# A fused attention and maxout kernel: evictions and filler dealt by engine clocks, q and k of batch 1 turned on TensorE

## The chip, the core and the metric

The kernel runs on one core of a Trainium2 chip. The core has TensorE (PE in the profile; its weight loads are PEld), VectorE (DVE), ScalarE (ACT), GpSimd (POOL) and SyncE (SP). Matrix products go from SBUF through TensorE into PSUM banks, and VectorE or ScalarE copies ("evicts") them to SBUF. SP's queue issues nearly all DMAs in program order. The metric is device time in microseconds (us). Three runs of the kernel before gave 203.61, 203.33 and 203.15 us, a median of 203.33 us.

## The reference

Attention with a causal mask over 4 batches, 8 heads, 768 positions and a head size of 64. Each head is either a full ("retrieval") head or a streaming head that sees 4 sink positions and a window of 64. The result goes through a maxout layer.

```python
scores = scale * np.matmul(q, k.transpose(0, 1, 3, 2))
scores = np.where(mask[None], scores, -1e9)      # causal, or causal & (sink | window)
a = np.exp(scores - scores.max(-1, keepdims=True))
a = a / (a.sum(-1, keepdims=True) + 1e-9)
x = np.matmul(a, v).transpose(0, 2, 1, 3).reshape(B * S, H * D)   # 3072 x 512
h1, h2 = x @ w1, x @ w2                          # 512 x 1024 each
out = np.maximum(h1, h2) @ w_out                 # 3072 x 512
```

## The kernel before, in words

**Pairs and chunks.** Two heads of one batch make a pair: 16 pairs, n = 0 to 15, four per batch (HP = 4). A pair's causal 6x6 block triangle is cut into six chunks (`CHUNKS`), so there are 96 chunks, t = 6n + c. For a chunk, `scores` (L282, matmuls at L296) fills one buffer of two PSUM banks, `expo` (L317) takes the exponential on ScalarE, `mask` (L328, from batch 1 on) multiplies on VectorE, and `weighted` (L348, matmuls at L359) multiplies with v. Five chunks of a pair have exponentials over 128x1024; c = 3 has 128x256. There are two score buffers, so the scores of chunk t+2 wait for the exponential of chunk t. When half a pair is complete, `normalise` (L368) divides on VectorE into the tile `x`.

**q, k, v.** `load_pair` (L189) issues three loads of 384 KB on SP's queue. q and k are cast to bf16 (`cast_qk`, L253) and transposed into `qkt`. This is done in one of two ways. `turn` (L209) makes six transposes on TensorE into a PSUM bank and one eviction. `turn_qk` (L262, the DMA at L267) is one DMA transpose on SP's queue. Pairs below `LONG` (L134, HP + 2 = 6) take the first way and also load q and k with six rows of a head side by side per partition (L183); pairs from 6 on take the second and load in rows of 64 elements (L176). `x` of batch 0 is transposed by TensorE, `x` of batches 1 to 3 by DMA (`turn_x`, L277).

**The maxout layer** uses max(h1, h2) = h2 + relu(h1 - h2): `w12` = w1 - w2 (`diff_w`, L565) and `w2o` = w2 @ w_out are formed on the chip. For each half of a batch (384 positions) `up` (L389, matmuls at L394) is one of eight units of 4 matmuls with an eviction into `g` (relu, L163 on VectorE, L167 on ScalarE), and `down` (L401, matmuls at L411) is one of three units of 12 matmuls with an eviction into `ot` and a store (L419). `w2o` needs `w2t`, the transpose of w2: eight units `prep_w2t` (L536) of four transposes and an eviction, and four units `prep_w2o` (L545).

**Order.** The schedule is written out by the program itself (`manual_schedule`); each engine executes its instructions in that order. Batch 0 runs through 24 chunks. Then come the sixteen `up` units of batch 0 with the eight `prep_w2t` between them (L707 to L734), while TensorE turns q and k of pair 4. Then a loop (L757 on) takes two chunks per step, "a group": scores of t+2 and t+3, `expo(t+2)`, `weighted` of t-2 and t-1, `side(t)`, half a budget of filler, `expo(t+3)`, `mask(t+2)`, `side(t+1)`, the other half of the filler, `mask(t+3)`.

**Side work.** `side` (L643) issues loads, casts, turns and DMA transposes at fixed chunks. For pairs that are turned on TensorE in this part: the casts at c = 5 two pairs ahead (q on VectorE, k on GpSimd), and the two turns at c = 0 and c = 1 of the pair before. For the others: both casts on GpSimd at c = 2 and `turn_qk` at c = 4, both two pairs ahead. From batch 1 on a `load_pair` is issued four pairs ahead at c = 4 or three ahead at c = 0, and `turn_x` of the previous pair at c = 4 (or c = 0), just ahead of `turn_qk`.

**Filler.** `fill` (L497) runs queued units until a budget of TensorE time is used: `cost()` of what is queued, divided by the groups left, where the first pair of the next batch counts as part of a batch's groups. `step` (L476) chooses between `turns`, `shorts` (`up`) and `longs` (`prep_w2o`, `down`, in four parts). Two PSUM banks serve them; a bank counts as free again `EVACUATED` = 1.1 us of planned TensorE time after its unit.

**Who evicts.** `evac` (L157) takes VectorE when the sum of estimated VectorE times given so far is not above that of ScalarE. `vec` and `sca` add to these sums, and L706 sets both to zero where batch 0's attention ends.

Of the kernel before, what the change touches and what calls it, by code (L numbers as in the profile page):

```python
# [49 lines left out]
def kernel(  # L50
# [82 lines left out]

    LONG = HP + 2  # L134
    NV = 3
# [10 lines left out]

    given = {"v": 0.0, "s": 0.0}

    def vec(us):
        given["v"] += us  # L150
        return nc.vector

    def sca(us):
        given["s"] += us
        return nc.scalar

    def evac(out, in_, cols, relu=False, on_vector=None):  # L157
        if on_vector is None:
            on_vector = given["v"] <= given["s"]
        if on_vector:  # L160
            eng = vec(0.16 + cols / 960)
            if relu:
                eng.tensor_scalar_max(out=out, in0=in_, scalar1=0.0)  # L163
            else:
                eng.tensor_copy(out=out, in_=in_)  # L165
        else:
            sca(0.2 + cols / 1300).activation(  # L167
                out=out, in_=in_, func=ACT.Relu if relu else ACT.Copy
            )

# [146 lines left out]
    def expo(t):  # L317
        n, c = chunk(t)
        s = st[n]
        w = 128 * len(CHUNKS[c][0])  # L320
        at = atp.tile([128, 2, 4, 128], BF16, tag="at", name="at")
        sca(0.13 + 2 * w / 1300).activation(  # L322
            out=at.rearrange("p h e c -> p h (e c)")[:, :, 0:w],
            in_=s["ps", c][:, :, 0:w], func=ACT.Exp, scale=scale,
        )
        s["at", c] = at

    def mask(t):  # L328
# [19 lines left out]
    def weighted(t):  # L348
        n, c = chunk(t)
        s = st[n]  # L350
        at = s["at", c]
        for hh in range(2):
            for e, (j, i) in enumerate(CHUNKS[c][0]):
                half, col = divmod(i, 3)
                first = ("po", half) not in s
                if first:
                    s["po", half] = psum_o.tile([128, 2, 3, D + 1], F32, tag="po", name="po")
                rhs = s["vb"][:, hh, j, :] if i - j < 2 else s["vf"][:, hh, j, :]
                nc.tensor.matmul(  # L359
                    s["po", half][:, hh, col, :], lhsT=at[:, hh, e, :], rhs=rhs,  # L360
                    start=first, stop=(c == done(n, half)),
                    skip_group_check=True,
                )
# [4 lines left out]
    def normalise(n, half):  # L368
        s = st[n]
        po = s["po", half]  # L370
        if half == 0:
            s["x"] = work.tile([128, NB, 2, D], BF16, tag="x", name="x")
        rez = work.tile([128, 2, 3], F32, tag="rez", name="rez")
        vec(0.2).reciprocal(out=rez, in_=po[:, :, :, D])  # L374
        vec(0.55).tensor_tensor(  # L375
            out=s["x"][:, 3 * half:3 * half + 3].rearrange("p i h d -> p h i d"),
# [61 lines left out]
    PART = 3  # L438
    plan = {"pe": 0.0, "owe": 0.0}
    free = [0.0, 0.0]  # L440
    busy = [False, False]
    turns, shorts, longs = [], [], []
    current = []
    EVACUATED = 1.1

    def spend(us):
        plan["pe"] += us

# [4 lines left out]
    def run_short(queue):  # L453
        e = pick_bank()
        us, f, _ = queue.pop(0)
        spend(us)
        f((bank_a, bank_d)[e])
        free[e] = plan["pe"] + EVACUATED
        return us

    def run_long():
        if not current:
            e = pick_bank()
            busy[e] = True
            current.extend([longs.pop(0), e, 0])
        (us, f, _), e, part = current
        spend(us)
        f(part, (bank_a, bank_d)[e])
        current[2] += 1
        if current[2] == 12 // PART:  # L470
            busy[e] = False
            free[e] = plan["pe"] + EVACUATED
            current.clear()
        return us

    def step():  # L476

        e = pick_bank()
        open_ = e is not None and free[e] <= plan["pe"]
        pend = [u[2] for u in longs] + ([current[0][2]] if current else [])  # L480
# [54 lines left out]

    def prep_w2t(fc, bank):  # L536
        pw = bank("pw").bitcast(BF16)[:, 0:512]
        for kc in range(KC):
# [3 lines left out]
            )  # L542
        evac(w2t[:, fc, :], pw, 270)

# [136 lines left out]
    for t in range(T0):  # L681
        if t + 2 < T0:
            scores(t + 2)
            expo(t + 2)
            spend(0.8)
        if t > 0:
            weighted(t - 1)
            spend(0.4)
        if t + 1 < T0:
# [25 lines left out]
    for n in range(HP + 1, HP + 4):  # L715
        load_pair(n)
    n = HP
    for e, u in enumerate(first_ups):
        u[1](banks.pop(0))
        if e == 1:  # L720
# [28 lines left out]
    longs += downs(0, 0) + downs(0, 1)  # L749
    scores(T0)  # L750
    scores(T0 + 1)
    expo(T0)
    expo(T0 + 1)
    mask(T0)
    mask(T0 + 1)
    for t in range(T0, T + 2, 2):
        b, p = pairs[min(t, T - 1) // NCH]  # L757
        if t + 2 < T:
            scores(t + 2)
            scores(t + 3)  # L760
            expo(t + 2)
            spend(0.7)
        if t > T0:
            weighted(t - 2)
            weighted(t - 1)
            spend(0.5)
        if t >= T:
# [91 lines left out]
```

## Time and profile before

The profiled execution took 203.91 us; its span is 202.1 us.

| engine | busy us | share of the span |
|---|---|---|
| PE | 187.7 | 93% |
| ACT | 112.3 | 56% |
| DVE | 108.5 | 54% |
| PEld | 105.5 | 52% |
| POOL | 67.9 | 34% |

TensorE's mean granted clock is 0.983. DMA moved 37.09 MB. In the chain of work that ended last, PE has 63%, DMA 16% and ACT 8% of the span.

How to read it: a row of the timeline has a start, a duration (of several instructions together, with "xN"), the engine, the line, the operation, out<-in, and in square brackets the idle time of the engine before it and what ended that. Rows of SP are DMA issues: their duration is the time SP's queue spent on the issue, waits included, and not the transfer. A row of the windows has a stretch, its length, then the busy time of PE, PEld, DVE, ACT and POOL with the number of instructions, the granted clock of TensorE, the share of the DMA engines and GB/s. A row of the grouped lines has the busy time and the mean ns of one, then the idle time ahead.

### The profile page before, as it was taken

Reading aid. Unit: us, or ns where it says so; the run is one execution under the profiler, and the core shown is the slowest. Engines: PE = TensorE matmul, PEld = TensorE weight load, DVE = VectorE, ACT = ScalarE, POOL = GpSimd, SP = SyncE. Lnnn points to the kernel's source line nnn. Section 1 sums busy time; section 2 is a strip of 40 time slices with the busy share of each in tenths; the row PEclk is TensorE's granted clock in tenths of the full one; section 3 lists DMA queues with packets and bytes.
Section 4 is the critical chain, followed back from the end, with each engine's and each line's share of the span. In section 5 each row is a group of like instructions: output and inputs, shape, how many; then the busy total and the mean of one; then the engine's idle time right before and its main releaser. Section 6 shows DMA issues by size and latency. Waiting matters only on the chain.

```text
span 202.1 us, 4504 instructions
## 1 busy us (share of the span) xinstructions
PE 187.7 (93%) x1856; PEld 105.5 (52%) x1856; DVE 108.5 (54%) x205; ACT 112.3 (56%) x151; POOL 67.9 (34%) x74
## 2 busy tenths in 40 slices
PE   7799998997999999579999999999999999999993
PEld 2366665575455555354555455554555645554452
DVE  1767667986776775826383737664623632232110
ACT  2789895589667667661747455935454630532110
POOL 1478349981764451507154242070200000000000
PEclk9999999999999999967999999999999999999999
DMA  6999999999999999999999999991703204100222
GB/s 208 299 292 334 388 351 301 170 206 196 224 209 171 221 212 222 248 233 228 236 202 243 193 264 151 180 224 56 169 3 107 74 17 143 52 3 0 104 104 104
DMA packets 91078, 37.09 MB, mean 183 GB/s; under 512 B 81074, under 2 KB 87474, under 8 KB 91058
## 3 DMA queue, kind: packets, MB, share of 16 engines
q1 hardware_dynamic: 89728, 35.33, 79.3%
q0 software_dynamic: 1040, 1.05, 3.6%
q10 hardware_dynamic: 290, 0.43, 0.8%
q8 instruction: 14, 0.23, 0.5%
q14 instruction: 6, 0.05, 0.1%
HBM read 25.46 MB, written 6.29 MB: 157 GB/s over the span
## 4 chain that ended last, share of the span: by engine, by line
PE 63%; DMA 16%; ACT 8%; SPq 3%; DVE 3%; issue 3%; POOL 2%; ACTq 0%; POOLq 0%; DVEq 0%
PE pout L411 24%; PE ph L394 20%; DMA kn<-in_k_dram 11%; PE ps L296 7%; PE po L359 7%; ACT at L322 6%; DMA qn<-in_q_dram 3%; PE ps L311 2%; SPq L267 2%; DMA qkt<-qk 2%; PE pt L214 1%; POOL qk L260 1%; PE pout L813 1%; ACT qkt L167 1%; SPq L176 1%
## 5 line engine op out<-in xcount | busy, mean ns | idle before, releaser
L322 ACT ACTIVATE at<-ps 128x1024 bf16<-128x1024 f32 x96 | 83.4, 918 | 36.2 <-PE ps L296 34.1
L394 PE MATMUL ph<-xt,w 128*128 128x384 bf16 x256 | 49.1, 329 | 1.2 <-DVE w L567 0.5
L411 PE MATMUL pout<-wob,g 128*128 128x512 bf16 x184 | 47.1, 384 | 0.0
L296 PE MATMUL ps<-qkt 64*128 64x256 bf16 (+1 forms) x416 | 30.6, 256 | 7.7 <-ACT at L322 4.1
L163 DVE TENSOR_SCALAR g<-ph 128x384 bf16<-128x384 f32 x37 | 20.6, 556 | 27.3 <-PE ph L394 27.3
L394 PEld LDWEIGHTS <-w 128*128 128x128 bf16 x256 | 23.5, 98 | 16.6 <-issue 1.8
L359 PEld LDWEIGHTS <-at 128*128 128x128 bf16 x672 | 25.8, 99 | 8.9 <-issue 6.1
L296 PEld LDWEIGHTS <-qkt 64*128 64x128 bf16 x416 | 16.2, 95 | 24.7 <-issue 18.0
L411 PEld LDWEIGHTS <-g 128*128 128x128 bf16 x184 | 17.9, 99 | 19.6 <-issue 1.4
L340 DVE TENSOR_TENSOR at<-at,msk 128x1024 bf16<-128x1024 bf16 (+2 forms) x36 | 20.6, 582 | 8.4 <-ACT at L322 8.4
L202 POOL TENSOR_TENSOR vf<-vb,rj 128x520 bf16<-128x520 bf16 x16 | 18.2, 1140 | 20.5 <-PE po L359 19.8
L165 DVE COPY ot<-pout 128x512 f32<-128x512 f32 (+1 forms) x16 | 10.8, 673 | 26.7 <-PE pout L411 24.4
L411 PE MATMUL pout<-w2o,xt 128*128 128x512 bf16 x92 | 24.5, 378 | 0.2
L167 ACT ACTIVATE g<-ph 128x384 bf16<-128x384 f32 x27 | 13.3, 491 | 18.3 <-PE ph L394 18.2
L260 POOL CAST qk<-qn 128x768 bf16<-128x768 f32 x12 | 9.9, 824 | 30.2 <-DMA qn<-in_q_dram 26.6
L359 PE MATMUL po<-vb,at 128*128 128x65 bf16 x352 | 19.2, 195 | 0.0
L167 ACT ACTIVATE ot<-pout 128x512 f32<-128x512 f32 (+1 forms) x9 | 5.2, 573 | 24.9 <-PE pout L411 21.6
L375 DVE TENSOR_TENSOR x<-po,rez 128x384 bf16<-128x384 f32 x32 | 17.8, 557 | 1.7 <-DMA xt<-x 0.7
L200 POOL CAST vb<-vn 128x768 bf16<-128x768 f32 x16 | 15.7, 980 | 8.9 <-DMA vn<-in_v_dram 8.9
L359 PE MATMUL po<-vf,at 128*128 128x65 bf16 x320 | 18.3, 196 | 0.0
L260 POOL CAST qk<-kn 128x768 bf16<-128x768 f32 x14 | 12.3, 879 | 13.5 <-DMA kn<-in_k_dram 13.5
L374 DVE RECIPROCAL rez<-po 128x6 f32<-128x6 f32 x32 | 6.2, 193 | 19.4 <-PE po L359 19.2
(54 smaller groups left out, 126.8 us busy)
## 6 DMA issues: line engine op xcount, KB each, us to landing
qn<-in_q_dram SPq DMA_DIRECT2D x16, 384.0 KB, 4.4
kn<-in_k_dram SPq DMA_DIRECT2D x16, 384.0 KB, 5.6
vn<-in_v_dram SPq DMA_DIRECT2D x16, 384.0 KB, 6.6
out_dram<-ot SPq DMA_DIRECT2D x23, 256.0 KB, 2.3
w2f<-in_moe_w_dram SPq DMA_DIRECT2D x2, 1024.0 KB, 9.9
w1f<-in_moe_w_dram SPq DMA_DIRECT2D x4, 512.0 KB, 10.5
wob<-in_moe_w_out_dram POOLq DMA_DIRECT2D x1, 1024.0 KB, 12.4
tab<-mask_table ACTq DMA_DIRECT2D x1, 288.5 KB, 3.5
```

The source lines that it names most:

```text
L163: eng.tensor_scalar_max(out=out, in0=in_, scalar1=0.0)
L167: sca(0.2 + cols / 1300).activation(out=out, in_=in_, func=ACT.Relu if relu else ACT.Copy)
L200: eng.tensor_copy(out=vb[:, :, :, 0:D], in_=s["vn"])
L202: nc.gpsimd.tensor_tensor(out=vf, in0=vb[:, :, 0:4, :], in1=rj[:, 2 * p:2 * p + 2, :].unsqueeze(3).to_broadcast([128, 2, 4, D + 1]), op=AL ...
L260: eng.tensor_copy(out=s["qk"][:, e], in_=src.rearrange("p h n d -> p n h d"))
L296: nc.tensor.matmul(ps[:, hh, e * 128:(e + m) * 128], lhsT=s["qkt"][rows, 1, j * 128:(j + 1) * 128], rhs=s["qkt"][rows, 0, i * 128:(i + m) ...
L322: sca(0.13 + 2 * w / 1300).activation(out=at.rearrange("p h e c -> p h (e c)")[:, :, 0:w], in_=s["ps", c][:, :, 0:w], func=ACT.Exp, scale= ...
L340: eng.tensor_tensor(out=at, in0=at, in1=mk, op=ALU.mult)
L359: nc.tensor.matmul(s["po", half][:, hh, col, :], lhsT=at[:, hh, e, :], rhs=rhs, start=first, stop=(c == done(n, half)), skip_group_check=True,
L375: vec(0.55).tensor_tensor(out=s["x"][:, 3 * half:3 * half + 3].rearrange("p i h d -> p h i d"), in0=po[:, :, :, 0:D], in1=rez.unsqueeze(3) ...
L394: nc.tensor.matmul(ph, lhsT=w12[:, kc, fc * 128:(fc + 1) * 128], rhs=xts[b][:, kc, tg * GT:(tg + 1) * GT], start=(kc == 0), stop=(kc == KC ...
L411: nc.tensor.matmul(pout, lhsT=lhsT, rhs=rhs, start=(e == 0), stop=(e == len(steps) - 1),)
```

## The change

1. `LONG` becomes 2 * HP = 8: q and k of pairs 6 and 7 are loaded with six rows side by side, cast at c = 5 (q on VectorE), and turned by TensorE. The two DMA transposes of these pairs leave SP's queue; their loads stay in it.
2. The two sums and the planner's own TensorE time become three clocks, `clk`. Every scores, exponential, mask, weighted, normalise and eviction is booked on its engine's clock, no earlier than its input is ready. `evac` takes the engine that would finish first. A bank is free when its booked eviction ends, in place of 1.1 us. The reset after batch 0 is gone.
3. The last `up` of batch 0 and the last three `prep_w2t` no longer run ahead of the first scores of batch 1. They are held back: the `up` runs between the scores of chunks T0 and T0 + 1, the three `prep_w2t` after those, with their evictions on VectorE.

```diff
-    LONG = HP + 2
+    LONG = 2 * HP
...
+    def book(e, us, ready):
+        clk[e] = max(clk[e], ready) + us
+        return clk[e]
...
     def evac(out, in_, cols, relu=False, on_vector=None):
+        ready = clk["pe"] + HOP
+        us_v, us_s = 0.16 + cols / 960, 0.2 + cols / 1300
         if on_vector is None:
-            on_vector = given["v"] <= given["s"]
+            on_vector = max(clk["v"], ready) + us_v <= max(clk["s"], ready) + us_s
+        clk["evac"] = book(*(("v", us_v) if on_vector else ("s", us_s)), ready)
...
     def scores(t):
+        clk["pe"] = max(clk["pe"], exp_end.get(t - 2, 0.0) + 0.06)
+        spend(0.1 + 0.06 * len(CHUNKS[c][0]) + (0.3 if n < HP and CHUNKS[c][1] else 0.0))
...
-        sca(0.13 + 2 * w / 1300).activation(
+        exp_end[t] = mask_end[t] = book("s", 0.13 + 2 * w / 1300, clk["pe"] + HOP)
...
-        eng = vec(0.1 + m * 0.15)
+        mask_end[t] = book("v", 0.1 + m * 0.15, exp_end[t])
...
     def run_short(queue):
-        spend(us)
+        clk["pe"] = max(clk["pe"], free[e]) + us
         f((bank_a, bank_d)[e])
-        free[e] = plan["pe"] + EVACUATED
+        free[e] = clk["evac"] + 0.06
...
-    given["v"] = given["s"] = 0.0
...
+    late = first_ups.pop()[1]
     for e, u in enumerate(first_ups):
...
-    prep_w2t(6, banks.pop(0))
-    prep_w2t(7, banks.pop(0))
...
     scores(T0)
+    expo(T0)
+    spend(0.65)
+    late(bank_o)
     scores(T0 + 1)
-    expo(T0)
     expo(T0 + 1)
+    for fc, bank in ((5, bank_a), (6, bank_d), (7, bank_o)):
+        prep_w2t(fc, bank, on_vector=True)
     mask(T0)
     mask(T0 + 1)
```

More of the change, by code (lines that the diff above doesn't have):

```diff
@@ L143, with spend @@
     st = [{} for _ in pairs]
-    given = {"v": 0.0, "s": 0.0}
+    clk = {"pe": 0.0, "v": 0.0, "s": 0.0}
+    HOP = 0.2
+    exp_end, mask_end = {}, {}
+    def spend(us):
+        clk["pe"] += us
+    def book(e, us, ready):
+        clk[e] = max(clk[e], ready) + us
+        return clk[e]
     def vec(us):
-        given["v"] += us
+        book("v", us, clk["pe"])
         return nc.vector
     def sca(us):
-        given["s"] += us
+        book("s", us, clk["pe"])
         return nc.scalar
     def evac(out, in_, cols, relu=False, on_vector=None):
+        ready = clk["pe"] + HOP
+        us_v, us_s = 0.16 + cols / 960, 0.2 + cols / 1300
         if on_vector is None:
-            on_vector = given["v"] <= given["s"]
+            on_vector = max(clk["v"], ready) + us_v <= max(clk["s"], ready) + us_s
+        clk["evac"] = book(*(("v", us_v) if on_vector else ("s", us_s)), ready)
         if on_vector:
-            eng = vec(0.16 + cols / 960)
             if relu:
-                eng.tensor_scalar_max(out=out, in0=in_, scalar1=0.0)
+                nc.vector.tensor_scalar_max(out=out, in0=in_, scalar1=0.0)
             else:
-                eng.tensor_copy(out=out, in_=in_)
+                nc.vector.tensor_copy(out=out, in_=in_)
         else:
-            sca(0.2 + cols / 1300).activation(
-                out=out, in_=in_, func=ACT.Relu if relu else ACT.Copy
-            )
+            nc.scalar.activation(out=out, in_=in_, func=ACT.Relu if relu else ACT.Copy)
     def load_one(n, name, src, eng):
@@ L373, in normalise @@
         rez = work.tile([128, 2, 3], F32, tag="rez", name="rez")
-        vec(0.2).reciprocal(out=rez, in_=po[:, :, :, D])
-        vec(0.55).tensor_tensor(
+        book("v", 0.74, clk["pe"] + HOP)
+        nc.vector.reciprocal(out=rez, in_=po[:, :, :, D])
+        nc.vector.tensor_tensor(
             out=s["x"][:, 3 * half:3 * half + 3].rearrange("p i h d -> p h i d"),
@@ L466, in run_long @@
         (us, f, _), e, part = current
+        if part == 0:
+            clk["pe"] = max(clk["pe"], free[e])
         spend(us)
@@ L471, in run_long @@
             busy[e] = False
-            free[e] = plan["pe"] + EVACUATED
+            free[e] = clk["evac"] + 0.06
             current.clear()
@@ L478, in step @@
         e = pick_bank()
-        open_ = e is not None and free[e] <= plan["pe"]
+        open_ = e is not None and free[e] <= clk["pe"]
         pend = [u[2] for u in longs] + ([current[0][2]] if current else [])
@@ L534, in load_columns, with prep_w2t @@
         nc.sync.dma_start(out=dst[:, :, cols], in_=a[:, :, cols])
-    def prep_w2t(fc, bank):
+    def prep_w2t(fc, bank, on_vector=None):
+        spend(0.23)
         pw = bank("pw").bitcast(BF16)[:, 0:512]
@@ L542, in prep_w2t @@
             )
-        evac(w2t[:, fc, :], pw, 270)
+        evac(w2t[:, fc, :], pw, 270, on_vector=on_vector)
     def prep_w2o(kc, part, bank):
```

15 lines of the change are left out of this document (7 added, 8 removed).

## The prediction

> **What bounds the kernel now.** I read the page first (busy times and the clock in 40 slices), then the waits of TensorE, then windows of 2 us around the largest of them, then the chain and SP's timeline behind it.
>
> ```profile
> PE 187.7 (93%) x1856; PEld 105.5 (52%) x1856; DVE 108.5 (54%) x205; ACT 112.3 (56%) x151; POOL 67.9 (34%) x74
> ...
> PEclk9999999999999999967999999999999999999999
> ```
>
> ```profile
> 87.07 1.03 PE L296 MATMUL ps<-qkt 64*128 64x256 bf16 x10 [2.82 <-DMA qkt<-qk]
> ```
>
> TensorE is busy for 93% of the span, so most of what is saved elsewhere is worth nothing. The exceptions are where TensorE itself stands or runs slowly. The largest single wait is the row of the timeline: before the first scores of pair 9 it stood for 2.82 us until the DMA transpose of that pair's q and k had landed. The two low digits of the clock stand just behind it. The windows:
>
> ```profile
> 60.00:70.00 10.00, 10.00 (x123) 5.40 (x121) 7.69 (x15) 6.82 (x8) 3.94 (x4) 1.00 1.17 198
> ```
>
> ```profile
> 84.00:86.00 2.00, 0.25 (x2) 0.00 (x0) 1.35 (x3) 0.76 (x1) 0.82 (x1) 1.00 0.97 192
> ...
> 90.00:92.00 2.00, 2.00 (x20) 1.39 (x21) 0.87 (x3) 0.85 (x2) 0.59 (x1) 0.50 1.33 233
> ```
>
> At 60 to 70 us TensorE is full at clock 1.00. At 84 to 86 it works 0.25 of 2 us, and at 90 to 92 its clock is 0.50. The chain from there gives the price, as the same groups of matmuls stand in it at both clocks:
>
> ```profile
> 83.10 3.92 DMA qkt<-qk
> ...
> 90.00 0.99 PE po L359 x16
> 90.99 1.28 PE ph L394 x4
> 92.27 2.11 PE pout L411 x6
> 94.38 0.65 PE ph L394 x4
> ...
> 95.58 0.60 PE po L359 x16
> ...
> 97.47 1.38 PE pout L411 x6
> ```
>
> 0.99 against 0.60, 1.28 against 0.65 and 2.11 against 1.38 us: the slow stretch costs 0.39 + 0.63 + 0.73 = 1.75 us (before 90 us the exponentials set the pace, so I count nothing there). The wait with its aftermath is 2.8 + 1.8 = 4.6 us.
>
> Why was that transpose late? SP's queue:
>
> ```profile
> 36.01 9.67 SPq L176 DMA_DIRECT2D kn<-in_k_dram  x1
> ...
> 53.44 3.36 SPq L267 DMA_TRANSPOSE qkt<-qk  x1
> ...
> 64.12 1.42 SPq L267 DMA_TRANSPOSE qkt<-qk  x1
> ...
> 79.16 2.52 SPq L419 DMA_DIRECT2D out_dram<-ot  x2
> 81.73 1.26 SPq L277 DMA_TRANSPOSE xt<-x  x1
> 83.10 2.17 SPq L267 DMA_TRANSPOSE qkt<-qk  x1
> ...
> 120.06 2.32 SPq L267 DMA_TRANSPOSE qkt<-qk  x1
> ```
>
> The queue is behind: the second store of 79.16 and the transpose of x at 81.73 (pair 6) had their data earlier, by these rows of VectorE:
>
> ```profile
> 74.52 0.56 DVE L375 TENSOR_TENSOR x<-po,rez 128x384 bf16<-128x384 f32 x1
> ...
> 76.28 0.68 DVE L165 COPY ot<-pout 128x512 f32<-128x512 f32 x1
> ```
>
> x was complete at 75.08 and ot at 76.96, and yet the transpose of pair 9 was issued at 83.10.
>
> **The change part by part.** The sum is made against the profiled execution, 203.91 us (span 202.1 and 1.8 around it), 0.58 above the median.
>
> *Transposes off SP's queue: -4.6 us.* The rows of 53.44 and 64.12 are the turns of pairs 6 and 7; they go, 3.36 + 1.42 = 4.78 us of the queue. What is queued behind them moves up until something else holds it: the last store before pair 9's turn needs ot at 76.96, then half of the 2.52 us of two stores, 1.26 us for x, so pair 9's turn is issued at about 79.5, and with the 3.92 us of its row it lands at 83.4. TensorE ran dry about 2.82 us before 87.07, at 84.25. So the wait goes, by 0.8 us; if no store stands between, by more. The loads of pairs 6 and 7 change shape in the same queue; the 9.67 us of a kn issue at 36.01 is one of them. I count nothing for them: they are issued ahead of the turn of 53.44, and pair 9 comes two loads later. I take the whole 2.8 + 1.8; the ends are 0 and -4.6.
>
> The Trainium skill ("TensorE: Matmul & The Clock Gate", section "HAM oscillation — how this bites in real kernels") puts the limit for idle gaps at about 3.4 us. This trace shows the half clock after a gap of 2.82 us. By that rule the slow stretch would not be the gap's doing, and 1.8 of the 4.6 us would stay; by the rows it goes. I go by the rows.
>
> *Four turns on TensorE: +1.4 us.* The price of six transposes, and of a unit of `prep_w2t`, in the chain:
>
> ```profile
> 42.16 0.22 PE pw L539 x4
> ...
> 43.03 0.34 PE pt L214 x6
> ```
>
> 4 x 0.34 = 1.36 us, in groups where TensorE is full (60 to 70 us), so all of it is on the path. It is paid from the filler's budget, which is then dealt out over later groups; those next to pair 8 have idle TensorE time, so as little as 0.3 could be left. Beside it are four evictions and two casts of q, now on VectorE:
>
> ```profile
> L167 ACT ACTIVATE qkt<-pt 128x768 bf16<-128x768 bf16 x7 | 5.7, 808 | 3.8 <-PE pt L214 3.8
> ...
> L165 DVE COPY qkt<-pt 128x768 bf16<-128x768 bf16 x4 | 3.8, 950 | 0.6 <-PE pt L214 0.6
> ...
> L260 DVE CAST qk<-qn 128x768 bf16<-128x768 f32 x4 | 3.1, 777 | 0.6 <-DMA qn<-in_q_dram 0.5
> ```
>
> At most 4 x 0.95 + 2 x 0.78 = 5.4 us on two engines, over some 13 us, in which by the row of 60 to 70 they have 2.3 + 3.2 us free in 10. It fits, so I count nothing; if it does not, a turn's late eviction holds a bank, some 0.5 us each, +2.0 at the far end.
>
> *Held-back units around the first scores: -1.2 us.*
>
> ```profile
> 47.35 0.39 PE L296 MATMUL ps<-qkt 64*128 64x256 bf16 x4
> ...
> 48.15 0.40 PE L296 MATMUL ps<-qkt 64*128 64x128 bf16 x6 [0.40 <-ACT w2t L167]
> ...
> 49.06 0.40 PE L296 MATMUL ps<-qkt 64*128 64x256 bf16 x4 [0.52 <-ACT at L322]
> ...
> 49.98 0.23 PE L296 MATMUL ps<-qkt 64*128 64x128 bf16 x2 [0.52 <-ACT at L322]
> ...
> 50.15 0.51 PE L214 MATMUL pt<-tab,qk 128*128 128x128 bf16 x6
> ```
>
> The three waits are 1.44 us. The moved work is 0.65 + 3 x 0.22 = 1.31 us, and it runs in them instead of ahead of them. With the `up` and the `prep_w2t` behind the scores of T0, the scores of T0 + 2 come 0.3 + 0.65 + 0.3 + 0.66 us after them, longer than one exponential. What is left is a short wait for the eviction of pair 4's k, which now has less work behind it, and one for the second exponential. I take -1.2; the ends are -0.4 and -1.8 (the waits, with the exponential no longer queued behind two evictions of w2t). The three evictions on VectorE stand ahead of the masks; the first `weighted` that needs a mask comes one group later.
>
> *Evictions dealt by three clocks: +1.0 us.* With both engines idle the rule takes ScalarE for every long eviction: 0.2 + cols/1300 is below 0.16 + cols/960 from 150 columns on. The eviction of a unit in the first half of the filler then stands in ScalarE's order ahead of `expo(t+3)`, which the model has not booked yet. Before pair 9 the sums sent these to VectorE. One case:
>
> ```profile
> 79.00 1.94 ACT L322 ACTIVATE at<-ps 128x1024 bf16<-128x1024 f32 x2 [1.09 <-PE ps L296]
> ...
> 80.28 0.69 DVE L165 COPY ot<-pout 128x512 f32<-128x512 f32 x1 [2.43 <-PE pout L411]
> ...
> 80.83 0.45 PE L296 MATMUL ps<-qkt 64*128 64x256 bf16 x6
> ```
>
> ```profile
> L167 ACT ACTIVATE ot<-pout 128x512 f32<-128x512 f32 x8 | 4.8, 597 | 21.6 <-PE pout L411 21.6
> ```
>
> On ScalarE it runs 80.28 to 80.88, so the second exponential ends at 81.8 in place of 80.94, and the second scores of 80.83 (from 81.1) wait 0.7 us. Six `down` units fall into the 15 groups up to pair 9; if half of them finish there and their groups give them half of that, it is 3 x 0.35 = 1.0 us. The ends are 0 and ten such evictions (the turns' too), 7 us. I stay near the low end, as batches 2 and 3 have such cases already at no wait:
>
> ```profile
> 96.86 0.49 ACT L167 ACTIVATE g<-ph 128x384 bf16<-128x384 f32 x1 [0.38 <-PE ph L394]
> ...
> 97.25 1.02 ACT L322 ACTIVATE at<-ps 128x1024 bf16<-128x1024 f32 x1
> ...
> 98.79 0.61 PE L296 MATMUL ps<-qkt 64*128 64x256 bf16 x10
> ```
>
> The exponential came late by this eviction, and the scores at 98.79 show no wait: there the groups are longer.
>
> *Nothing:* batch 0 (its evictions are placed by hand, and its order stays) and the tail (evictions alternate there, and a unit of TensorE's takes longer than one).
>
> *The sum:* -4.6 + 1.4 - 1.2 + 1.0 = -3.4 us: 200.5 for the profiled execution, 199.9 for the median.
>
> **The rivals.**
>
> *The wait stays, or comes back (slower).* What is late next is pair 13's transpose: issued at 120.06, and TensorE would come for it 4.6 us earlier than before.
>
> ```profile
> 127.34 0.39 PE L296 MATMUL ps<-qkt 64*128 64x256 bf16 x4
> ```
>
> If it lands 4 to 5 us after its issue, it had 2 to 3 us to spare; the queue is ahead by some 3.6 us and TensorE by 4.6, so 1 to 2 us are left. If the queue gains nothing, the wait is back with its slow clock: -3.4 + 4.6 = +1.2, 204.5. It decides from about 1.6 us of waiting if the clock falls (1.6 + 1.8 = 3.4). For it speaks that the queue has hardly a gap; against it, the 4.78 us taken out.
>
> *A shorter wait.* One of the two transposes is late by 1 us, and the clock holds: 200.9. For it speaks the margin of 0.8 us above.
>
> *Evictions ahead of exponentials (slower).* At 0.7 us each, it decides from about six (-4.4 + 6 x 0.7); with seven it is 203.8. For it speaks the rule's lean to ScalarE, against it that an exponential already booked turns the choice to VectorE. The Trainium skill ("PSUM — Partial Sum Buffer", section "Engine vs sequencer instructions") says that ScalarE and VectorE queues are strict first-in first-out; by that rule the exponential cannot pass the eviction, and the rows of 96.86 and 97.25 agree.
>
> *The gap does not set the clock.* The slow stretch stays: -1.6, 201.7. This is what the rule in the Trainium skill ("TensorE: Matmul & The Clock Gate") would make of it.
>
> *The dealing changes nothing:* without the 1.0 it is 198.9, inside the forecast.
>
> **How the numbers follow.** Forecast 0.56, shorter wait 0.17, clock 0.05, wait whole 0.10, evictions 0.12. The forecast reaches from 203.33 - 2.8 - 1.8 - 1.8 + 0.3 = 197.2 to 201.9 (3 us of evictions). The range goes to 203.6, which leaves out the whole wait and the worse half of the evictions. A difference of 0.2% (0.4 us) is about what a measurement can tell. Faster: the first three, less 0.01 near the bound, 0.77; same 0.03; slower 0.20.
>
> **What would show it.** No row of TensorE waits over 1 us for the DMA of qkt, and the clock is 0.9 or more in all slices from the second on: right on the first term. A wait before pair 13: the rival. TensorE's waits for the exponentials between 50 and 84 us show the dealing: some 1 us is as forecast, over 4 makes it wrong. The waits among the first four scores should fall below 0.5 us. The transposes of the turns should be 24 more.

## The result, and the profile after

| | before | after |
|---|---|---|
| median of 6 runs, us | 203.07 (201.93 to 203.61) | 200.27 (199.89 to 200.75) |
| profiled execution, us (span) | 203.91 (202.1) | 200.75 (198.9) |
| mean granted clock of the profiled execution | 0.983 | 0.999 |

The ratio is 0.9872, with a 95% interval of 0.9841 to 0.9904: the change saves 1.3%. Ratios here leave out runs that lie over 1.5% above the fastest of their kernel, so where a kernel's runs scatter I give the median too.

The page of the kernel after, busy times and the clock in 40 slices:

```profile
PE 184.2 (93%) x1855; PEld 105.0 (53%) x1880; DVE 92.1 (46%) x177; ACT 129.3 (65%) x185; POOL 65.3 (33%) x72
...
PEclk9999999999999999999999999999999999999999
```

The 6 and 7 of before are gone from the clock. ScalarE has gone from 112.3 to 129.3 us of work, VectorE from 108.5 to 92.1: the three clocks deal to ScalarE. TensorE's waits, as sum, count and longest, in the kernel after:

```profile
PE ps L307 <- ACT at L334: 2.8, 9, 0.6
...
PE ps L307 <- DMA qkt<-qk: 1.0, 3, 0.4
```

Before, the wait for the transposes was a single one of 2.8 us. It has become three of 0.3 to 0.4 us, ahead of pairs 9, 10 and 13. Their rows of the timeline:

```profile
85.83 0.39 PE L307 MATMUL ps<-qkt 64*128 64x256 bf16 x4 [0.37 <-DMA qkt<-qk]
...
95.48 0.85 PE L307 MATMUL ps<-qkt 64*128 64x256 bf16 x10 [0.31 <-DMA qkt<-qk]
...
106.78 0.61 PE L307 MATMUL ps<-qkt 64*128 64x256 bf16 x10
...
124.64 0.67 PE L307 MATMUL ps<-qkt 64*128 64x256 bf16 x10 [0.35 <-DMA qkt<-qk]
```

Three rows of the kernel before fix the same points there:

```profile
55.28 0.61 PE L296 MATMUL ps<-qkt 64*128 64x256 bf16 x10
...
98.79 0.61 PE L296 MATMUL ps<-qkt 64*128 64x256 bf16 x10
...
109.10 0.61 PE L296 MATMUL ps<-qkt 64*128 64x256 bf16 x10
```

These are the first scores of pairs 5, 10 and 11; those of pair 9 stood at 87.07. Where the time went, by pairs: pair 9 is 1.24 us earlier. From pair 9 to pair 10 it was 11.72 us and is 9.65 (-2.07, the slow clock: in the order that the program writes out, TensorE has the same matmuls there). From 10 to 11 it was 10.31 and is 11.30 (+0.99, with three more matmuls of `down`). Pair 11 is 2.32 us earlier, and the last instruction 3.2 us; the 0.9 us gained behind pair 11 stand in no term of the forecast.

### The profile page after: what moved, and what is told of

Read it like the earlier page. It is cut to its first block, busy times and chain, and to the rows that moved or that the text cites. A ratio compares the mean times of both kernels' runs of the same rounds, so it can differ in the third digit from the quotient of the medians.

```text
span 198.9 us, 4522 instructions
## 1 busy us (share of the span) xinstructions
PE 184.2 (93%) x1855; PEld 105.0 (53%) x1880; DVE 92.1 (46%) x177; ACT 129.3 (65%) x185; POOL 65.3 (33%) x72
## 4 chain that ended last, share of the span: by engine, by line
PE 64%; SPq 9%; DMA 8%; ACT 6%; POOL 5%; issue 3%; DVE 3%; ACTq 0%
PE pout L427 27%; PE ph L410 17%; PE po L374 7%; PE ps L307 7%; SPq L192 6%; DMA w1f<-in_moe_w_dram 6%; ACT at L334 5%; POOL w2b L578 3%; PE pw L565 3%; DMA qkt<-qk 3%; SPq L541 2%; PE pout L828 1%; POOL w L582 1%; SPq L548 1%; PE pt L223 1%
## 5 line engine op out<-in xcount | busy, mean ns | idle before, releaser
L334 ACT ACTIVATE at<-ps 128x1024 bf16<-128x1024 f32 x96 | 85.0, 916 | 11.1 <-PE ps L307 8.7
L410 PE MATMUL ph<-xt,w 128*128 128x384 bf16 x256 | 48.3, 326 | 0.9 <-ACT ot L178 0.4
L427 PE MATMUL pout<-wob,g 128*128 128x512 bf16 x172 | 43.8, 379 | 0.7
L178 ACT ACTIVATE g<-ph 128x384 bf16<-128x384 f32 x53 | 26.0, 491 | 23.5 <-PE ph L410 23.2
L178 ACT ACTIVATE ot<-pout 128x512 f32<-128x512 f32 (+1 forms) x19 | 11.1, 586 | 24.5 <-PE pout L427 23.8
L211 POOL TENSOR_TENSOR vf<-vb,rj 128x520 bf16<-128x520 bf16 x16 | 17.4, 1090 | 27.9 <-PE po L374 27.3
L209 POOL CAST vb<-vn 128x768 bf16<-128x768 f32 x16 | 14.6, 911 | 11.1 <-DMA vn<-in_v_dram 10.2
L269 POOL CAST qk<-qn 128x768 bf16<-128x768 f32 x10 | 9.0, 905 | 26.0 <-DMA qn<-in_q_dram 23.3
L427 PEld LDWEIGHTS <-xt 128*128 128x128 bf16 x92 | 8.6, 97 | 9.3 <-issue 1.6
L178 ACT ACTIVATE qkt<-pt 128x768 bf16<-128x768 bf16 (+2 forms) x12 | 9.0, 755 | 4.3 <-PE pt L223 4.2
```

Source lines behind the costliest of these rows:

```text
L178: nc.scalar.activation(out=out, in_=in_, func=ACT.Relu if relu else ACT.Copy)
L209: eng.tensor_copy(out=vb[:, :, :, 0:D], in_=s["vn"])
L211: nc.gpsimd.tensor_tensor(out=vf, in0=vb[:, :, 0:4, :], in1=rj[:, 2 * p:2 * p + 2, :].unsqueeze(3).to_broadcast([128, 2, 4, D + 1]), op=AL ...
L269: eng.tensor_copy(out=s["qk"][:, e], in_=src.rearrange("p h n d -> p n h d"))
L334: nc.scalar.activation(out=at.rearrange("p h e c -> p h (e c)")[:, :, 0:w], in_=s["ps", c][:, :, 0:w], func=ACT.Exp, scale=scale,)
L410: nc.tensor.matmul(ph, lhsT=w12[:, kc, fc * 128:(fc + 1) * 128], rhs=xts[b][:, kc, tg * GT:(tg + 1) * GT], start=(kc == 0), stop=(kc == KC ...
```

## The experiments

Each was timed in five rounds against the kernel before. The theory: pair 9's transpose is late in SP's queue, its wait makes TensorE's clock fall, and the turns on TensorE mend both. The rivals are those of the prediction.

### One part alone

The turns alone:

```diff
-    LONG = HP + 2
+    LONG = 2 * HP
```

> The kernel before with q and k of pairs 6 and 7 turned on TensorE and nothing else. Theory (the late DMA transpose and the slow clock behind it are most of the gain): -4.6 for the wait before pair 9 and its slow stretch, +1.4 for four turns, so about -3.2 us, no wait over 1 us on a DMA of qkt, and a clock of 1.0 from 80 to 96 us. Rival (the queue gains nothing): the wait stays and the turns are paid, +1.4 us.

Measured 200.42 us (199.94 to 202.76), ratio 0.990 (0.9844 to 0.9955): the theory's figure. Compared with the 203.32 us of the kernel before beside it, it is -2.9. The one run at 202.76 was the profiled one, and its clock fell elsewhere; I come back to it below.

The held-back units alone:

```diff
+    late = first_ups.pop()[1]
...
-    prep_w2t(6, banks.pop(0))
-    prep_w2t(7, banks.pop(0))
...
     scores(T0)
+    expo(T0)
+    late(bank_o)
     scores(T0 + 1)
-    expo(T0)
     expo(T0 + 1)
+    for fc, bank in ((5, bank_a), (6, bank_d), (7, bank_o)):
+        prep_w2t(fc, bank, on_vector=True)
```

> The kernel before with the held-back units around batch 1's first scores and nothing else. Theory (pair 9's transpose goes by SP's queue, whatever TensorE does before it): the first groups come about 0.8 us earlier and the wait before pair 9 grows by as much, so 0 us, within 0.4. Rival (the gain is kept): -0.8 to -1.2 us.

Measured 203.04 us (201.21 to 204.92), ratio 0.9992 (0.9954 to 1.0031): no difference. Its timeline says where the gain went:

```profile
86.68 0.61 PE L296 MATMUL ps<-qkt 64*128 64x256 bf16 x10 [3.91 <-DMA qkt<-qk]
```

TensorE comes to pair 9 earlier and waits for the same transpose: 3.91 us in place of 2.82.

The three clocks alone; the whole of the change at `book`, `evac` and the planner, with `LONG` and the order of the first scores as before:

```diff
-            on_vector = given["v"] <= given["s"]
+            on_vector = max(clk["v"], ready) + us_v <= max(clk["s"], ready) + us_s
```

> The kernel before with the evictions dealt by the three clocks and nothing else. Theory (evictions ahead of exponentials cost some 1 us up to pair 9, which that pair's wait takes up): 0 us, within 0.5, with the wait before pair 9 some 1 us shorter. Rival A (the dealing itself gains): -1 us or more. Rival B (it costs in every group): +1 us or more.

Measured 201.66 us (200.3 to 204.43), ratio 0.9941 (0.9901 to 0.9981): faster, where its theory had 0 within 0.5. By the medians (-1.7 beside 203.32) it is the figure of rival A, that the dealing itself gains. In its profile the clock is at full speed throughout, and the wait is short:

```profile
79.35 0.61 PE L307 MATMUL ps<-qkt 64*128 64x256 bf16 x10
...
86.75 0.61 PE L307 MATMUL ps<-qkt 64*128 64x256 bf16 x10 [1.29 <-DMA qkt<-qk]
```

Pair 8's scores are 0.8 us later than the 78.57 of before:

```profile
78.57 0.61 PE L296 MATMUL ps<-qkt 64*128 64x256 bf16 x10
```

Of these, 0.46 us stand at pair 5 already (55.74 against 55.28). From pair 5 to the point where TensorE runs dry before pair 9 it takes 29.72 us in place of 28.97, with the same matmuls by the program's order. So the dealing does cost time ahead of pair 9, as forecast, but here that only uses up the wait. The clock was down less often: five of its twelve runs had a mean clock of 0.998 or more, three about 0.991, four 0.983. That the shorter gap is the reason fits, and is not shown by itself. At full clock its five runs average 201.15 us, those of the kernel before 201.56 (12 runs), so some 0.4 us of rival A's gain is left that the clock does not explain.

### One part undone

Without the turns; the diff is against the changed kernel:

```diff
-    LONG = 2 * HP
+    LONG = HP + 2
```

> The changed kernel with the DMA transposes of pairs 6 and 7 back (dealing and held-back units stay). Theory (pair 9's transpose lands when SP's queue lets it; the clock falls with the length of TensorE's gap): the wait before pair 9 is back at about 2 us, the clock falls in some runs, 202.5 us, 2 us above the changed kernel. Rival (the queue's relief is not needed once the dealing fills the gap): within 0.5 us of the changed kernel.

Measured 202.8 us (201.66 to 203.95), ratio 1.0006 (0.9978 to 1.0034). The wait is back at 2.10 us, and none of its twelve runs had a mean clock above 0.992:

```profile
86.54 0.61 PE L307 MATMUL ps<-qkt 64*128 64x256 bf16 x10 [2.10 <-DMA qkt<-qk]
```

Without the turns nothing is left of the gain.

Without the three clocks, with all of the sums of before:

```diff
-            on_vector = max(clk["v"], ready) + us_v <= max(clk["s"], ready) + us_s
+            on_vector = given["v"] <= given["s"]
```

> The changed kernel with evictions and banks dealt by the sums of before (turns and held-back units stay). Theory of the prediction (the dealing costs about 1 us by evictions ahead of exponentials): 199.3 us, 1 us under the changed kernel. Rival A (it costs nothing): within 0.4 us of it, 200.3. Rival B (the dealing carries part of the gain, as it did alone): 201 us or more.

Measured 199.51 us (198.9 to 200.99), ratio 0.9851 (0.9808 to 0.9895). By the medians the dealing costs 0.8 us beside the other two parts; the intervals of the two kernels overlap, and the profiled spans (199.2 here, 198.9 with the dealing) don't show it.

Without the held-back units:

```diff
-    late = first_ups.pop()[1]
...
+    prep_w2t(6, banks.pop(0))
+    prep_w2t(7, banks.pop(0))
...
     scores(T0)
-    expo(T0)
-    spend(0.65)
-    late(bank_o)
     scores(T0 + 1)
+    expo(T0)
     expo(T0 + 1)
-    for fc, bank in ((5, bank_a), (6, bank_d), (7, bank_o)):
-        prep_w2t(fc, bank, on_vector=True)
```

> The changed kernel with the last up and three prep_w2t ahead of batch 1's first scores again. Theory (the gaps among the first scores cost 0.8 us, and now and then the clock behind them): 0.8 us above the changed kernel, 201.1, with a mean clock of 0.992 in some runs. Rival (what is won there is lost at pair 9): within 0.3 us of it.

Measured 200.66 us (199.62 to 201.26), ratio 0.9909 (0.9872 to 0.9946): by the medians the part is worth 0.4 us in the changed kernel. The waits among the first scores stand again in its timeline:

```profile
49.10 0.40 PE L307 MATMUL ps<-qkt 64*128 64x256 bf16 x4 [0.59 <-ACT at L334]
...
50.01 0.23 PE L307 MATMUL ps<-qkt 64*128 64x128 bf16 x2 [0.52 <-ACT at L334]
```

### Does the gap set the clock?

The kernel before, with matmuls that nobody uses in the gap; SP's queue is left as it was.

```diff
+        if t == NCH * 9 - 2:
+            pz = (bank_a, bank_d)[pick_bank()]("pz")
+            idle(13, pz)
         if t + 2 < T:
             scores(t + 2)
```

> The kernel before with 13 matmuls of zeros (13 x 0.216 = 2.8 us) ahead of the scores of pair 9, into a bank that nobody reads; they do no work and fill the wait. Theory (the idle gap is what halves the clock): the clock stays at 1.0 from 84 to 96 us, the scores of pair 9 still start when the transpose has landed, and the kernel is 1.8 us faster. Rival (the clock falls for another reason, or a gap under 3.4 us does not count): the clock falls all the same and the time is within 0.4 us of before.

```profile
84.53 2.97 PE L608 MATMUL pz<-zero 128*128 128x512 bf16 x13
...
87.43 0.61 PE L296 MATMUL ps<-qkt 64*128 64x256 bf16 x10
...
97.04 0.61 PE L296 MATMUL ps<-qkt 64*128 64x256 bf16 x10
```

Pair 9 starts 0.36 us later than before, and pair 10 all the same 1.75 us earlier (98.79 before). By the program's order TensorE has the same matmuls between the two, so the difference is the clock: it stays at full speed over the whole span. But pair 9's transpose was issued at 81.47 in this profile, 1.63 us earlier than in that of before. With the 3.92 us of its row there it would have landed at about 85.4 (an estimate), so pair 9 waited for the unused matmuls, and without them the gap in this execution would have been about 0.9 us and not 2.82. One profile against one profile does not show the cause, then; the runs do.

The median is 202.32 us (201.67 to 203.73), 1.0 below the kernel before beside it, and the ratio 1.0016 (0.9976 to 1.0056), which is within the rival's 0.4 us. So the -1.8 of the expectation is in the runs only in part. None of the twelve was at the 0.983 or below that 17 of 29 runs of the kernel before beside them had. Seven had a full clock and lie at 202.3 or below; they average 202.0, against 201.6 for the kernel before at full clock, so the filling has a price of its own. The other five had a mean clock of about 0.99 and lie at 203.0 or above. In those five the clock fell somewhere; no profile of them shows where. The kernels with the turns alone and with the stores on GpSimd (below) show one such place in their profiles, at 50 to 55 us.

### Evictions ahead of exponentials

The changed kernel, with every eviction of the filler's first half, which stands ahead of `expo(t+3)`, put on VectorE:

```diff
+        if on_vector is None and clk.get("hold"):
+            on_vector = True
...
+        clk["hold"] = True
         fill(0.5 * budget)
+        clk["hold"] = False
```

> The changed kernel with every eviction of the first half of a group's filler on VectorE, so that none stands ahead of the group's second exponential on ScalarE. Theory (such evictions hold up the second scores of the next group): the waits and gaps at the second scores of pairs 6 and 7 go, and the kernel is 0.5 to 1 us faster than the changed one, 199.5. Rival (the filler takes the time up): within 0.3 us of it.

Measured 200.83 us (199.78 to 201.93), ratio 0.9909 (0.9874 to 0.9944): not better, against the theory's 199.5, and 0.6 us above the changed kernel, where the rival had it within 0.3. Between 50 and 84 us no exponential makes TensorE wait any more, but an eviction does, and the transposes of pairs 9 and 10 make it wait longer than in the changed kernel. The waits of 50 to 84 us, and two rows behind them:

```profile
PE pw L567 <- DVE qkt L178: 1.4, 1, 1.4
```

```profile
86.41 0.77 PE L309 MATMUL ps<-qkt 64*128 64x256 bf16 x10 [0.90 <-DMA qkt<-qk]
...
96.58 0.61 PE L309 MATMUL ps<-qkt 64*128 64x256 bf16 x10 [1.07 <-DMA qkt<-qk]
```

So taking the evictions away from ahead of the exponentials gains nothing. As this run brings waits of its own, it does not show by itself what the dealing costs.

### How much has to leave the queue?

Pair 6 alone turned on TensorE:

```diff
-    LONG = HP + 2
+    LONG = HP + 3
```

> The kernel before with pair 6 alone turned on TensorE (LONG = HP + 3), pair 7 still by DMA. Theory (what counts is the time taken out of SP's queue): half the effect of both pairs. Of the 4.78 us of the queue the 3.36 us of pair 6's row go; the wait before pair 9 falls from 2.8 us to 0.2 to 1.2 us, the clock holds mostly, and with two turns (0.7 us) on TensorE the time is 200.5 to 201.5. Rival (it is the transpose right ahead, pair 7's, that delays pair 9's): the wait stays above 2 us and the time is 202.8 to 203.8.

Measured 199.95 us (199.46 to 200.7), ratio 0.9869 (0.9823 to 0.9915): better than the theory's 200.5 to 201.5, and against the rival. One pair gives the whole effect. Its wait before pair 9 is 0.44 us, and every run had a clock of 0.998 or more:

```profile
85.84 0.61 PE L296 MATMUL ps<-qkt 64*128 64x256 bf16 x10 [0.44 <-DMA qkt<-qk]
```

Pair 8 as well, on top of the turns and the held-back units with the old sums:

```diff
-    LONG = 2 * HP
+    LONG = 2 * HP + 1
```

> The changed kernel without the three clocks (old sums deal the evictions), and pair 8 turned on TensorE as well (LONG = 2 HP + 1). Theory (with pairs 6 and 7 out of SP's queue its lateness is paid for; one more pair saves at most the 0.4 us waits before pairs 9 and 10 and costs two turns of 0.34 us): 199.5 to 200.1, not better than with LONG = 2 HP (199.5). Rival (each pair taken out of the queue goes on paying): 198.5 or less.

Measured 201.25 us (200.31 to 201.97), ratio 0.9924 (0.9891 to 0.9956). The direction is the theory's, the size is not: 1.7 us above 199.51, where two turns cost 0.7. The windows show TensorE less full ahead of pair 9, though no transpose is late; the first line is this kernel's, the second that of the kernel with `LONG` = 2 * HP and the old sums:

```profile
76.00:86.00 10.00, 8.91 (x119) 5.09 (x116) 6.05 (x12) 6.73 (x9) 3.48 (x4) 1.00 0.69 162
```

```profile
76.00:86.00 10.00, 9.73 (x119) 5.26 (x118) 5.88 (x13) 6.95 (x10) 4.20 (x5) 1.00 1.25 240
```

The first has two waits for exponentials in this stretch, 0.63 us ahead of the scores at 80.25 and 0.46 ahead of those at 84.44; the second has no wait over 0.2. They are more than the 0.82 us between the two lines. What makes these exponentials late is not settled.

### The queue, or what stands behind it?

The kernel before, with batch 0's stores issued by GpSimd:

```diff
-        nc.sync.dma_start(out=out[row:row + 128, :], in_=ot)
+        (nc.gpsimd if b == 0 else nc.sync).dma_start(out=out[row:row + 128, :], in_=ot)
```

> The kernel before, with the stores of batch 0's output issued by GpSimd's queue in place of SP's; pairs 6 and 7 are still turned by DMA, and evictions and units are as before. Theory (pair 9's transpose is late because it stands in SP's queue behind other issues, whichever they are): without the two stores of 79.16 us (2.52 us) and those ahead of them it is issued 2.5 us or more earlier, the wait of 2.8 us before pair 9's scores falls below 1 us, the clock stays at 0.9 or more in all slices, and the time falls by 2 to 3 us, to 200.3 to 201.3. Rival (the DMA engines are behind, not the queue): the same bytes move, the wait stays at 2.3 us or more and the time within 0.6 us of the kernel before. Second rival: the stores wait for ot on GpSimd and hold up its casts of q and k; then the wait before pair 9 goes to the casts, and the time is not better.

Measured 205.53 us (204.38 to 206.64), ratio 1.0143 (1.0087 to 1.0198): slower, and neither the theory nor its first rival. SP's queue and VectorE ahead of pair 9:

```profile
79.34 3.01 SPq L277 DMA_TRANSPOSE xt<-x  x1
82.46 2.46 SPq L267 DMA_TRANSPOSE qkt<-qk  x1
```

```profile
83.71 3.61 DVE L340 TENSOR_TENSOR at<-at,msk 128x1024 bf16<-128x1024 bf16 x2
```

```profile
84.67 0.83 POOL L260 CAST qk<-qn 128x768 bf16<-128x768 f32 x1
...
86.21 0.83 POOL L200 CAST vb<-vn 128x768 bf16<-128x768 f32 x1
```

```profile
87.38 0.20 PE L359 MATMUL po<-vb,at 128*128 128x65 bf16 x1 [1.17 <-DVE at L340]
```

With the stores gone from the queue, the transpose of x was taken up at 79.34, 2.39 us earlier and so nearly the stores' 2.52; but its issue took 3.01 us in place of 1.26, and pair 9's turn came only 0.64 us earlier. So the time of an issue that is taken out need not reach what stands two places behind it. What lengthened the issue of x no run tells. Nor could pair 9's turn have gone much earlier: the casts of its q and k, held up on GpSimd, ended at 81.53. TensorE no longer waited for that transpose, because it had waited 1.17 us for the second of two masks that took 3.61 us together, and 0.50 us more for x. Its clock fell behind these waits, and at 50 to 55 us as well. The second rival had GpSimd's casts held up by the stores and pair 9 waiting for the casts; the stores did hold them up, but it was VectorE that TensorE waited for.

### A version that beats both

Pair 6 alone on TensorE, with the held-back units as in the run of that part alone, and the old sums:

```diff
-    LONG = HP + 2
+    LONG = HP + 3
...
+    late = first_ups.pop()[1]
```

> The kernel before with pair 6 alone turned on TensorE (LONG = HP + 3) and the units held back around batch 1's first scores; the old sums deal the evictions. Theory (the parts add up: pair 6 alone gave 199.95 us, and holding back takes 0.5 to 0.8 us off where the clock holds): 199.1 to 199.6 us, clock 1.00, the wait before pair 9 at most 1 us. Rival (TensorE comes to pair 9 earlier by what holding back saves, and with only two turns in its way the wait before pair 9 grows by the same): 199.8 us or more, wait before pair 9 of 1 us or more, and in part of the runs a clock below 0.995.

Measured 199.12 us (199.04 to 199.47), ratio 0.9814 (0.9764 to 0.9864), all clocks 0.997 or more. The parts add up. The rival's wait is there in small:

```profile
85.44 0.61 PE L296 MATMUL ps<-qkt 64*128 64x256 bf16 x10 [0.76 <-DMA qkt<-qk]
```

## Why the prediction was right, point by point

The forecast was 200.5 us for the profiled execution and 199.9 for the median; measured are 200.75 and 200.27, inside the likeliest case. The sum was right, in part by luck. The turns alone gave -2.9 us where their two terms had -3.2. The held-back units and the dealing were both taken too large, -1.2 and +1.0, and the two errors cancel: from the turns alone (200.42) to the whole change (200.27) it is -0.15, where the forecast had -0.2.

**Transposes off SP's queue, -4.6.** The largest term, and the deciding one: the turns alone gave -2.9 with their own cost of 1.4 in it, and without them the gain is gone. That this gap brings the clock down is shown by the runs with the filled gap: none of twelve was at 0.983 or below, where 17 of 29 were without the filling. What it is worth is less sure than the 1.8 of the term, as their median is 1.0 us lower. In the profile of the changed kernel the stretch from pair 9 to 10 gained 2.07 us with the same matmuls.

What failed in it is the step "pair 9's turn is issued at about 79.5". The row of the kernel after:

```profile
76.60 3.39 SPq L435 DMA_DIRECT2D out_dram<-ot  x2
80.08 1.83 SPq L286 DMA_TRANSPOSE xt<-x  x1
82.02 1.46 SPq L276 DMA_TRANSPOSE qkt<-qk  x1
```

It was issued at 82.02, and its q and k were used at 85.83. The queue did gain 2.56 us up to the stores (76.60 against 79.16). There I had the last store wait for ot at 76.96, an eviction of before; in the kernel after that eviction itself is later:

```profile
79.01 0.60 ACT L178 ACTIVATE ot<-pout 128x512 f32<-128x512 f32 x1 [0.38 <-PE pout L427]
```

It ends at 79.61, the store at 79.99, and x and pair 9 follow. The queue is no longer behind there: from 63.60 to 69.52 us it issued nothing, as a store waited for its ot. (Such a wait for data stands between SP's rows, not in their durations.) A time taken from the trace of before was used as fixed for work that the change itself delays. The forecast margin of +0.8 us was a wait of 0.37. The wait of 2.82 us was closed from both sides: 1.24 us because the transpose landed earlier, and the other 1.2 because TensorE came later (at 85.46 in place of 84.25, the wait taken off both).

**Turns on TensorE, +1.4.** The count is as forecast, 24 more transposes (before, then after):

```profile
L214 PE MATMUL pt<-tab,qk 128*128 128x128 bf16 x72 | 6.0, 219 | 0.5 <-DVE sink L627 0.4
...
L223 PE MATMUL pt<-tab,qk 128*128 128x128 bf16 x96 | 8.0, 219 | 0.7 <-DVE sink L642 0.4 <-DVE qk L269 0.2
```

From pair 5 to pair 9, without the wait, it was 28.97 us (87.07 - 2.82 - 55.28) and is 30.27, +1.3. Pair 5 of the kernel after:

```profile
55.19 0.61 PE L307 MATMUL ps<-qkt 64*128 64x256 bf16 x10
```

These 1.3 us are not simply the price of the turns. By the program's order one part of `down`, three matmuls, has left this stretch for the one from pair 10 to pair 11; at 1.38 us for six (the row of 97.47) that is an estimated 0.7 us, and it is found again in the +0.99 there. The four turns less this part would be 0.7. Nor do the two terms add up: over the same stretch the turns alone took 30.18 us (57.54 to 87.72), +1.2, the dealing alone 29.72, +0.75, and both together +1.3, where the sum had 2.4. Pair 6 alone, two turns and no part of `down` moved, took 30.46 (54.94 to 85.40), +1.5. So the size came out, but not as a price by the transpose, and what the rest is no run tells. By the medians the time with pair 6 alone turned was 0.5 us lower than with both (0.2, each against the kernel before beside it): the second pair's turns bought nothing.

Besides, pair 9 still waits 0.37 us for its transpose. So its start is set by that transpose, and what TensorE does ahead of it counts only as far as it fills the wait or holds up what the queue waits for; the forecast added it up in full.

**Held-back units, -1.2.** Right in sign, too large. The waits among the first four scores are gone, as forecast. The kernel after:

```profile
47.23 0.39 PE L307 MATMUL ps<-qkt 64*128 64x256 bf16 x4 [0.18 <-DVE qkt L176]
...
48.31 0.40 PE L307 MATMUL ps<-qkt 64*128 64x128 bf16 x6
...
49.42 0.70 PE L307 MATMUL ps<-qkt 64*128 64x256 bf16 x6
```

Measured it is 0.4 us by undoing it, 0.9 between the kernel without the dealing and the turns alone, 0.8 with pair 6 alone, and nothing where pair 9's wait is still there. The term mis-sized is the sum of the three waits, 1.44 us, of which I let 1.2 reach the end; 0.4 to 0.9 did. Alone the whole of it went into pair 9's wait; where the rest went in the changed kernel, no run tells.

**Dealing by three clocks, +1.0.** By the medians it is +0.8 us against the same kernel with the old sums and +0.2 without the held-back units (200.66 against the 200.42 of the turns alone); on its own it was a gain. So the term was too large, and its mechanism is not what the runs show. Evictions do stand between exponentials, as argued. Of the kernel after:

```profile
60.65 1.02 ACT L334 ACTIVATE at<-ps 128x1024 bf16<-128x1024 f32 x1
61.64 0.81 ACT L178 ACTIVATE qkt<-pt 128x768 bf16<-128x768 bf16 x1
62.34 2.85 ACT L334 ACTIVATE at<-ps 128x1024 bf16<-128x1024 f32 x3
```

```profile
63.41 0.40 PE L307 MATMUL ps<-qkt 64*128 64x128 bf16 x6 [0.19 <-ACT at L334]
```

The eviction puts the exponential back by 0.8 us, and TensorE loses 0.19, as its filler covers the rest. All waits for exponentials between 50 and 84 us, before and then after:

```profile
PE ps L296 <- ACT at L322: 1.0, 2, 0.5
```

```profile
PE ps L307 <- ACT at L334: 0.4, 2, 0.2
```

Some 1 us was to be the sign of being right, but the kernel before has that much itself, and the change made it less. The "0.7 us each" was the far end of that price. What the dealing then costs stays open: part of it is in the waits for transposes (1.0 us in the kernel after, 0.4 without the dealing), but the two profiled spans are equal within 0.3 us.

**The rivals.** The wait came back whole nowhere in the changed kernel. The shorter wait, with the clock held (200.9), came true in part: three waits of 0.3 to 0.4 us. Pair 13, named as next, is one of them. Evictions ahead of exponentials fell by the last point. "The gap does not set the clock" fell by the runs with the filled gap, with the limit that in five of the twelve the clock fell once all the same. "The dealing changes nothing" is nearly so: 0.2 to 0.8 us.

## What to carry to other kernels

When work is moved to the engine that is full in order to make a late transfer early, the work itself fills part of the wait; count both sides, and move the least that brings the wait under the gap that costs clock: one pair did here what two did. Times that a queue waits for, such as an eviction, move with the change, so follow them into the changed order and don't take them from the old trace. And a gain ahead of a wait that stays is worth nothing: the same held-back units gave 0 alone and 0.8 us once the transpose was early.

## What the runs showed of the hardware

**The clock falls in portions.** Over the 78 runs of the kernel before that were timed beside the experiments, the mean granted clock lay near one of four values, and the time went with it: 201.6 us on average at 0.996 and above (12 runs), 202.5 near 0.991 (31), 203.8 near 0.983 (32), 204.5 near 0.975 (3). A step of 0.0083 over a span of 202 us is 1.7 us of lost clock, at half speed 3.4 us of slow stretch, and it costs 0.7 to 1.3 us. In the profiled execution of before, the windows of 86 to 88 and 92 to 94 us bound the stretch:

```profile
86.00:88.00 2.00, 0.93 (x10) 0.54 (x10) 0.28 (x1) 0.28 (x1) 0.00 (x0) 0.74 1.06 262
...
92.00:94.00 2.00, 2.00 (x6) 0.72 (x5) 1.16 (x2) 0.00 (x0) 1.11 (x2) 0.55 1.43 218
```

At 0.74 the half clock began 1.04 us before 88, at 0.55 it ended 1.8 us behind 92: 6.8 us, two portions. The Trainium skill ("TensorE: Matmul & The Clock Gate", section "What's actually happening") describes a free-running window of about 3.4 us over which the activity is watched; the portions agree with that length. Its rule that a whole idle window is needed does not: gaps of 2.82 and 2.10 us brought the half clock here, and in the kernel with the turns alone there was no wait above 0.52 us ahead of it. That kernel's windows:

```profile
48.00:50.00 2.00, 1.08 (x15) 0.65 (x15) 1.75 (x3) 2.00 (x4) 1.63 (x2) 1.00 1.14 260
50.00:52.00 2.00, 1.26 (x11) 0.77 (x10) 1.71 (x3) 1.76 (x3) 1.27 (x2) 0.77 1.09 341
52.00:54.00 2.00, 2.00 (x6) 0.58 (x7) 1.15 (x3) 0.00 (x0) 0.00 (x0) 0.50 1.36 231
```

TensorE was busy for 2.34 of the first 4 us there, in pieces, and the clock fell behind them. It was one of six runs. With the stores on GpSimd it worked 1.95 of the 4 us from 84 to 88, with no wait above 1.17 us, and the clock fell to 0.50 behind that too. But the kernel before has the same three waits among its first scores, and TensorE was busy for 1.96 of 3.4 us in both profiles (47.40 to 50.80 before, 48.04 to 51.44 with the turns alone); before, its clock held there. That several short gaps close together can do what one long gap does is the reading. The gaps alone don't decide it, and what does, no run here measured.

**A mask beside GpSimd's casts lasts until they end.** With the stores on GpSimd its three casts ran back to back from 84.67 to 87.04 us, and two masks on VectorE, begun at 83.71, took 3.61 us together, to 87.32; one of the same shape takes 0.69 us in the kernel before:

```profile
88.78 0.69 DVE L340 TENSOR_TENSOR at<-at,msk 128x1024 bf16<-128x1024 bf16 x1 [2.49 <-ACT at L322]
```

Two more such rows of casts in the run with the stores moved, 71.34 to 73.71 and 97.96 to 100.32 us, each had a mask of 128x256 beside them. It took 2.91 us from 70.94 and 2.96 us from 97.51, both to some 0.15 us behind the last cast; the same shape took 0.28 us at 79.02 and 88.70 in this run, with no cast beside it. In the kernel before, a single cast of v from 51.57 to 52.94 us had this one beside it, which ends at 53.07:

```profile
52.16 0.91 DVE L340 TENSOR_TENSOR at<-at,msk 128x256 bf16<-128x256 bf16 x1
```

In the grouped lines the 36 mask operations took 821 ns each with the stores moved (first row), 582 before (second):

```profile
L340 DVE TENSOR_TENSOR at<-at,msk 128x1024 bf16<-128x1024 bf16 (+2 forms) x36 | 29.3, 821 | 7.3 <-ACT at L322 7.3
```

```profile
L340 DVE TENSOR_TENSOR at<-at,msk 128x1024 bf16<-128x1024 bf16 (+2 forms) x36 | 20.6, 582 | 8.4 <-ACT at L322 8.4
```

The Trainium skill ("GPSIMD Engine Reference", section "1. Specifications") says that GpSimd shares its way into SBUF with VectorE and contends with VectorE's instructions of two SBUF inputs, which a mask is; the rows agree. That the casts are the cause is read from where the masks end; no run took the casts away.
